# Filter rows and length-64 results fetched for four residues at a time, in a fused spectral filter and MLP-mixer kernel

## The chip, the cores and the metric

The kernel runs on one core of a Trainium2 chip. The metric is the device time of one execution in microseconds (us). TensorE multiplies matrices and accumulates in PSUM; VectorE and ScalarE do elementwise work and can read PSUM; GpSimd does elementwise work in SBUF and issues DMAs; SyncE (SP) only issues DMAs. Each engine works through its own instructions in order and waits on semaphores for the others.

## The reference

The input x has 8 batches of 3008 rows and 256 columns, all in fp32. First each column is filtered in the frequency domain, then a mixer with a token part and a channel part follows:

```
X = rfft(x, axis=1)                      # 1505 frequencies
y = irfft(X * (filt_r + 1j*filt_i), n=3008, axis=1)
h = relu(y^T @ w_tok1) @ w_tok2          # over the 3008 rows: 3008 -> 256 -> 3008
u = y + h^T
out = u + relu(u @ w_ch1) @ w_ch2        # over the columns: 256 -> 1536 -> 256
```

The weights of the mixer come in as 64-bit floats and are turned into fp32 inside the kernel.

## The kernel before

**The transform.** 3008 = 47 x 64, so a transform of length 3008 is done as one of length 64 over rows that lie 47 apart, and one of length 47 for each of its residues. Because the data are real, only the residues k2 = 0 to 31 (with 32 beside 0) are computed. The length-64 result of a batch goes to DRAM (`z_d`). For each residue, z is read back with the 47 positions folded to two halves of 24 rows, multiplied by a small table (`wbi_t`), multiplied by the complex filter rows of that residue, multiplied by a second table, and written to DRAM (`g_d`), from where the mixer reads it.

**Batches.** `GROUPS` holds each batch alone. Batch 0 goes first in a form of its own (`first`), with TensorE to itself. The steps of every later batch b + 1 are generated by `dft` (L561) and woven into the mixer of batch b: `mix` (L1150) yields after each piece of its work, and the loop at the end of the kernel asks a fixed table of places when to take the next step of `dft` (each of which stops at a `yield`). So the order of every engine's instructions is written out by hand and does not depend on times. Batch 1 takes its length-64 transform in twelve plain matmuls; batches 2 to 7 (`tiled`) use sums and differences made by VectorE.

**One length-47 step.** From batch 1 on, a step handles two pairs of residues, that is four residues (`per` is 2, `KC` is 2). `b_pair` (L707) does 16 small matmuls through `four` (L523), eight for each pair, into two PSUM banks. `products` (L715) multiplies both banks by the filter on VectorE, two operations for each bank, one for each pair, since the filter rows of each pair lie in a tile of their own (L721). `join` adds the products to a complex result. `bi_pair` (L729) does the second 16 matmuls, one step later, and SP stores the result. Between the steps lies other work of the mixer. There are eight such steps a batch, seven batches.

**Buffers and SP's order.** `filts` is a ring of three tiles of 128 partitions by 2 (real, imaginary) by 2 by 256. The transform of x uses all of each tile; `filt_pair` (L221) uses only half of it, `[:, :, 0, :]`, with the two residues of the pair in partitions 0 to 63 and 64 to 127. It issues eight DMAs of 24 or 23 rows (L226, L228). Rows between the loaded ones must be zero: `zero_rows` (L587) clears the used half by a memset on GpSimd (L588) when a batch's x is done. `t2_load` (L655) reads z for one pair, four DMAs, eight for the first pair (L667, L668); `w_load` is the table load (L584, one for both pairs) and then `filt_pair`. All of these stand in SP's queue. Ahead of batch 1's first step the order is: table and filter of pair 0, z of pair 0, filter of pair 1, z of pair 1, table and filter of pair 2, z of pairs 2 and 3. Inside the loop a step issues the z reads of the two pairs two steps ahead, and then the filter of pairs three and four ahead.

**The mixer around it.** An item of the channel part is one pair of hidden blocks for 512 rows. `up_first` (L998, matmuls at L1002) fills two banks, ScalarE copies one quarter (L1005), `up_middle` (L1008) adds on VectorE, `up_last` (L1014, matmuls at L1018) reuses the same banks once VectorE has read them, and `down` (L1025, matmuls at L1036) multiplies the item before. All their VectorE sums go through `v` (L979, so their line is L980). `w1_sums` (L819) is a set of GpSimd sums (L829) in the first mixer batch, beside batch 1's transform.

Of the kernel before, what the change touches and what calls it, by code (L numbers as in the profile page):

```python
# [22 lines left out]
D = 256  # L23
P = 128
# [9 lines left out]
XB = 2  # L34
XF = 2 * FB
KC = 2
WC = 2
TI = P - 2 * KH + 1
DT = 256
# [88 lines left out]
def kernel(  # L128
# [53 lines left out]
    def bank(tag):  # L182
        return (psg if tag == "pg" else psum).tile([P, 512], FP32, tag=tag, name="ps_" + tag)
# [34 lines left out]
    def raw(src, row, ap):  # L218
        return bass.AP(tensor=src.tensor, offset=src.offset + row * D, ap=ap)

    def filt_pair(c):  # L221
        t = filts[c % FB]
        for i, src in enumerate((filt_r, filt_i)):
            for odd in range(KC):
                k, to = c * KC + odd, odd * HALF
                nc.sync.dma_start(t[to:to + A, i, 0], raw(src, k, [[64 * D, A], [1, D]]))  # L226
                n, row = (A - 1, 64 - k) if k else (A, 32)
                nc.sync.dma_start(t[to + 32:to + 32 + n, i, 0], raw(src, row, [[64 * D, n], [1, D]]))  # L228

    def filt_load(c):  # L230
        t, k0 = filts_0[c % len(filts_0)], c * KC
# [329 lines left out]
    def dft(bs):  # L561
        first = bs[0] == 0
        nb = len(bs)
        tiled = bs not in GROUPS[0:2]
        per = 1 if first else 2 // nb
        todo = [(b, c) for b in bs for c in range(NXC // 2 if tiled else NXC)]
        wbs = {}
        kept = []
# [1 line left out]
        def table_load(c):  # L570
            if first:
                if c < 5:
                    where, tag = (t1p, "t1") if c > 2 else (wbp, "wb")
                    t = where.tile([P, 2 * P, WC], FP32, tag=tag, name="wb")
                    for h in range(2):
                        nc.gpsimd.memset(t[half_of(h), ts(1 - h, P)], 0.0)
                    kept.append(t)
                wbs[c] = kept[c % 5]
                for h in range(2):
                    nc.sync.dma_start(wbs[c][half_of(h), ts(h, P)], wbi0_d[half_of(h), c])  # L580
            else:
                if c % per == 0:
                    both = wbp.tile([P, per, 4, HALF], FP32, tag="wb", name="wb")
                    nc.sync.dma_start(both, wbi_d[:, c:c + per])  # L584
                    wbs.update((c + j, both[:, j]) for j in range(per))

        def zero_rows(c):  # L587
            nc.gpsimd.memset(filts[c][:, :, 0, :], 0.0)  # L588

        def w_load(c):  # L590
            table_load(c)
            (filt_load if first else filt_pair)(c)

        to_load = list(enumerate(todo))

# [54 lines left out]
                    v = turned.rearrange("p s d -> p d s")[:, d:d + 16, :]  # L650
                    nc.vector.transpose(v, v)
        t2s, t3s, prods = {}, {}, {}
        wide = per * nb

        def t2_load(c):  # L655
            if first:
                return
            if c % per == 0:
                both = t2p.tile([P, per, KC, nb, D], FP32, tag="t2", name="t2")
                t2s.update((c + j, both[:, j]) for j in range(per))  # L660
            for h in range(2):
                z = z_d[place_of[bs[0]][0]].rearrange("(e h k) a b d -> e h a k b d", e=2, h=2)
                for e in range(2):
                    to = t2s[c][ds(h * HALF + e * A, A)]
                    k = c == 0
                    if k:
                        nc.sync.dma_start(to[:, 0:1], z[h, e, :, 0:1])  # L667
                    nc.sync.dma_start(to[:, k:KC], z[e, h, :, c * KC + k:c * KC + KC])  # L668

        def b_unit(k):  # L670
            ps = bank("pg").rearrange("p (b d) -> p b d", b=2)[:, 0:nb, :]
# [25 lines left out]
                           in_=ps.rearrange("p b (g e i) -> p b g e i", e=DH, i=CW))  # L697

        def two_banks(tags):
            return [bank(tag).rearrange("p (b d) -> p b d", b=2)[:, 0:wide, :] for tag in tags]  # L700

        def of(j):
            return slice(j * nb, (j + 1) * nb)

        def b_pair(c):  # L707
            pss = two_banks(turn)
            for j in range(per):
                wb, t2 = wbs[c + j], t2s[c + j]  # L710
                four(lambda h, i: pss[h][half_of(i), of(j)], lambda h, i: wb[half_of(h, KH), i],
                     lambda h, i: t2[half_of(h, KH), i])
            return pss

        def products(c, pss):  # L715
            where = (p1p, p2p)
            for h in range(2):
                prods[c, h] = where[h].tile([P, 2, wide, D], FP32, tag="p%d" % (h + 1), name="p%d" % (h + 1))
                for j in range(per):
                    f = filts[(c + j) % FB][:, :, 0, :].unsqueeze(2).to_broadcast([P, 2, nb, D])  # L720
                    nc.vector.tensor_tensor(out=prods[c, h][:, :, of(j)], in1=f, op=ALU.mult,  # L721
                                            in0=pss[h][:, of(j)].unsqueeze(1).to_broadcast([P, 2, nb, D]))
# [6 lines left out]
        def bi_pair(c, tags):  # L729
            pss, p = two_banks(tags), prods.pop((c, 0))  # L730
            for j in range(per):
                wb = wbs[c + j]
                four(lambda i, h: pss[i][half_of(h), of(j)], lambda i, h: wb[half_of(i), 2 + h],
                     lambda i, h: p[half_of(i), h, of(j)])
            t3 = t3p.tile([P, per * KC, nb, D], FP32, tag="t3", name="t3")
            if per == 1:
                for i in range(KC):
                    by_block(t3[:, i], pss[i])
            else:
                for i in range(KC):  # L740
                    by_block(t3[:, i::KC, 0], pss[i])
            for h in range(2):
                nc.sync.dma_start(g_d[place_of[bs[0]][0]][ds(c * KC, per * KC), ts(h, KH)].rearrange("k r b d -> r k b d"),
                                    t3[half_of(h, KH)])

        if not first:
            for c in range(tiled, FB):
                zero_rows(c)
            for c in range(2 * per):
                if not tiled and c < FB:  # L750
                    w_load(c)
                t2_load(c)
                if tiled and 0 < c < FB:
                    w_load(c)
        yield "w"
        yield "b"
        if not first:
            last = K2 // KC
            for c in range(0, last, per):
                pss = b_pair(c)  # L760
                if c:
                    bi_pair(c - per, ("pg", "pg"))
                products(c, pss)
                for j in range(c + 2 * per, c + 3 * per):
                    if j < last:
                        t2_load(j)
                for j in range(c + min(2 * per, FB), c + min(2 * per, FB) + per):
                    if j < last:
                        w_load(j)
                yield "m"  # L770
                join(c)
                if c + per == last:
                    yield "i"
                    bi_pair(c, turn)
                if c + per < last:
                    yield "b"
            return
        if first:
            for i in range(2):
# [615 lines left out]
```

## Time and profile before

| what | value |
|---|---|
| median of 3 runs | 2410.55 us (2408.51 to 2411.98) |
| the profiled execution, its own time | 2411.46 us |
| its span | 2409.7 us |
| its mean granted TensorE clock | 0.994 |
| TensorE busy | 2363.4 us, 98% |
| VectorE busy | 1954.8 us, 81% |
| ScalarE, GpSimd busy | 689.2 us, 29%; 629.8 us, 26% |
| products with the filter, L721 | 224 operations of 128x512, 0.68 us each |
| filter loads of batches 1 to 7 | 896 DMAs of 24 or 23 KB from SP |
| z reads | 420 DMAs of 48 KB, 56 of 24 KB from SP |

All numbers after the median come from one execution. "Busy" is the sum of the time in which the engine had an instruction in work. A row of the trace in order of time has the start and the duration in us, the engine, the line, the operation, what is written and read, and how many instructions are merged; in square brackets stands how long the engine was idle before it and what released it. Rows of waits read: engine and what it was about to write, its line, what it waited for, us in total, times, longest. "PEld" is the weight load in front of a matmul, "SPq" and "ACTq" are issues of DMAs by SP and ScalarE. A matmul in fp32 appears as two records. The granted clock is the share of full speed that TensorE was given.

### The profile page before, as it was taken

To read this page: it belongs to the slowest core of one execution; us is meant where nothing else is said; L and a number is where in the kernel's file an instruction comes from. 1 tells how busy PE (TensorE), PEld (TensorE's weight loads), DVE (VectorE), ACT (ScalarE), POOL (GpSimd) and SP (SyncE) were. 2 spreads that over 40 slices of the span, in tenths; PEclk is the share of its full clock that TensorE was granted. 3 is DMA by queue.
4 is the path that set the end of the run, shared out by engine and by line. 5 is a ranking of instruction groups with operands and counts; after the bars stand their busy time and mean duration, and the time that the engine had idled before them with its cause. 6 is when DMAs were issued, how large, how long until landed. Compare 5 with 4: busy or idle time off the path is not lost.

```text
span 2409.7 us, 38162 instructions
## 1 busy us (share of the span) xinstructions
PE 2363.4 (98%) x13132; PEld 2013.6 (84%) x13132; DVE 1954.8 (81%) x3781; ACT 689.2 (29%) x1339; POOL 629.8 (26%) x1124
## 2 busy tenths in 40 slices
PE   7988999999999999999999999999999999999998
PEld 4666888888898888988888888988889888898887
DVE  7797887778877888778887788878888788877776
ACT  5732222222223222232222222222222322222222
POOL 7476433211221121112112311221121112112121
PEclk8999999999999999999999999999999999999999
DMA  9973446432353334533345333633235333331100
GB/s 216 234 202 109 137 129 221 126 113 82 112 187 125 90 101 127 182 107 98 101 136 173 105 99 96 196 113 113 86 115 182 122 98 105 111 129 32 39 14 21
DMA packets 195313, 294.37 MB, mean 122 GB/s; under 512 B 40030, under 2 KB 130548, under 8 KB 195120
## 3 DMA queue, kind: packets, MB, share of 16 engines
q1 hardware_dynamic: 153632, 231.26, 30.8%
q0 software_dynamic: 34688, 53.83, 8.4%
q10 hardware_dynamic: 6800, 6.85, 1.0%
q8 instruction: 104, 1.70, 0.3%
q14 instruction: 89, 0.73, 0.1%
HBM read 209.06 MB, written 82.72 MB: 121 GB/s over the span
## 4 chain that ended last, share of the span: by engine, by line
PE 91%; DVE 3%; DMA 2%; issue 1%; POOL 1%; ACT 1%; SPq 0%; DVEq 0%; ACTq 0%; POOLq 0%
PE ps_po L1036 35%; PE ps_pg L1002 20%; PE ps_pg L1018 15%; PE ps_b L523 4%; PE ps_b L866 3%; PE ps_acc L923 3%; PE ps_acc L866 2%; PE ps_pg L523 2%; PE ps_b L923 2%; PE ps_b L901 2%; PE ps_acc L901 2%; DMA st<-in_moe_w_tok_dram 1%; DMA filt<-in_filt_r_dram 1%; DMA x<-in_x_dram 1%; DVE both L279 1%
## 5 line engine op out<-in xcount | busy, mean ns | idle before, releaser
L1044 POOL DMA_DIRECT2D out_dram<-r x752 | 408.2, 550 | 1466.2 <-issue 780.3
L1023 ACT ACTIVATE hh<-hh 128x512 f32<-128x512 f32 (+1 forms) x576 | 347.7, 621 | 1015.7 <-DVE hh L980 1008.2
L980 DVE TENSOR_TENSOR hh<-ps_pg,s 128x512 f32<-128x512 f32 (+3 forms) x864 | 481.4, 585 | 169.3 <-ACT s L1005 159.2
L1036 PE MATMUL ps_po<-t,wc 128*128 128x256 f32 (+1 forms) x2296 | 558.8, 380 | 0.5 <-DVE t L980 0.4
L1036 PEld LDWEIGHTS ps_po<-t,wc 128*128 128x128 f32 x2296 | 427.2, 190 | 96.4 <-issue 39.1
L1002 PE MATMUL ps_pg<-v,wc 128*128 128x256 f32 (+1 forms) x1728 | 412.7, 375 | 1.5 <-POOL wc L381 1.5
L1036 PE MATMUL ps_po<-hh,wc 128*128 128x256 f32 (+1 forms) x1722 | 411.5, 375 | 0.6 <-POOL wc L382 0.6
L1002 PEld LDWEIGHTS ps_pg<-v,wc 128*128 128x128 f32 x1728 | 328.2, 190 | 39.8 <-POOL wc L381 2.3
L1036 PEld LDWEIGHTS ps_po<-hh,wc 128*128 128x128 f32 x1722 | 326.8, 190 | 38.4 <-POOL wc L382 1.4
L1018 PE MATMUL ps_pg<-u,wc 128*128 128x256 f32 (+1 forms) x1152 | 291.9, 376 | 2.5 <-DVE hh L980 2.4
L980 DVE TENSOR_TENSOR t<-t,hh 128x256 f32<-128x256 f32 (+1 forms) x576 | 247.6, 430 | 19.8
L1018 PEld LDWEIGHTS ps_pg<-u,wc 128*128 128x128 f32 x1152 | 216.9, 190 | 34.1 <-DVE hh L980 8.0
L980 DVE TENSOR_TENSOR s<-ps_pg,hh 128x512 f32<-128x512 f32 (+1 forms) x288 | 196.0, 681 | 31.1 <-DVE hh L980 1.4
L1005 ACT COPY s<-ps_pg 128x256 f32<-128x256 f32 (+1 forms) x288 | 105.9, 368 | 337.4 <-PE ps_pg L1002 333.9
L980 DVE TENSOR_TENSOR t<-hh 128x512 f32<-128x512 f32 (+1 forms) x288 | 194.2, 674 | 0.6 <-ACT hh L1023 0.6
L1002 PE MATMUL ps_pg<-u,wc 128*128 128x256 f32 (+1 forms) x576 | 169.9, 377 | 3.9 <-DVE hh L980 3.9
L1018 PE MATMUL ps_pg<-v,wc 128*128 128x256 f32 (+1 forms) x576 | 168.8, 375 | 0.0
L1002 PEld LDWEIGHTS ps_pg<-u,wc 128*128 128x128 f32 x576 | 108.4, 191 | 20.1 <-DVE hh L980 7.8
L1018 PEld LDWEIGHTS ps_pg<-v,wc 128*128 128x128 f32 x576 | 108.9, 190 | 12.9
L980 DVE TENSOR_TENSOR u<-ps_acc,u 128x256 f32<-128x256 f32 (+1 forms) x84 | 46.1, 549 | 71.5 <-PE ps_acc L923 50.5
L980 DVE TENSOR_TENSOR u<-ps_b,u 128x512 f32<-128x512 f32 (+2 forms) x126 | 74.4, 591 | 28.9 <-PE ps_b L923 26.7
L721 DVE TENSOR_TENSOR p<-ps_b,filt 128x512 f32<-128x512 f32 x112 | 72.3, 685 | 16.2 <-PE ps_pg L523 13.4
(164 smaller groups left out, 2700.8 us busy)
## 6 DMA issues: line engine op xcount, KB each, us to landing
w<-w_tmp SPq DMA_DIRECT2D x84, 448.0 KB
w<-w_tmp SPq DMA_DIRECT2D x35, 896.0 KB
out_dram<-r POOLq DMA_DIRECT2D x696, 32.0 KB, 3.8
g_tmp<-t SPq DMA_DIRECT2D x112, 192.0 KB
t<-g_tmp SPq DMA_DIRECT2D x42, 512.0 KB
t<-z_tmp SPq DMA_DIRECT2D x420, 48.0 KB
z_tmp<-t SPq DMA_DIRECT2D x72, 256.0 KB
wb<-wbi_t SPq DMA_DIRECT2D x56, 256.0 KB
```

Source lines behind the costliest of these rows:

```text
L523: nc.tensor.matmul(outs(i, j), stat(i, j), mov(i, j), start=True, stop=True)
L721: nc.vector.tensor_tensor(out=prods[c, h][:, :, of(j)], in1=f, op=ALU.mult, in0=pss[h][:, of(j)].unsqueeze(1).to_broadcast([P, 2, nb, D]))
L866: nc.tensor.matmul(ps[:, at], w[:, n], mov, start=(j == 0 and i in (0, 2)), stop=(j == AP - 1 and i >= 5))
L901: nc.tensor.matmul(ps[:, ds(q * P, n)], t4[b, c][:, r, ts(dh, P)], wai[:, 0:n], start=(first and q == 0), stop=(not first and q == 3))
L923: nc.tensor.matmul(ps[:, ds(j * hw, hw)], h1[:, n, :], w2m[m % 2][:, at, 0:hw], start=(i < 2 and j == 0), stop=(j == len(todo) - 1))
L980: nc.vector.tensor_tensor(out=out, in0=in0, in1=in1, op=op)
L1002: nc.tensor.matmul(ps[:, 0:hw], chan[0][:, jp, n, :], mov, start=True, stop=True)
L1005: nc.scalar.copy(out=s[:, 0], in_=g[0][:, 0, 0:hw])
L1018: nc.tensor.matmul(ps[:, 0:hw], chan[0][:, jp, n, :], mov, start=True, stop=True)
L1023: nc.scalar.activation(out=hs, in_=hs, func=AF.Relu)
L1036: nc.tensor.matmul(po[i][:, j, 0:hw], chan[1][:, jp, n, :], mov, start=(jp == 0 and first == 1), stop=(jp == JP - 1 and last == 1))
L1044: q.dma_start(bass.AP(tensor=ob.tensor, offset=ob.offset + row * D + g * cw, ap=[[N1 * D, 32], [D if h else -D, n], [1, cw]]), blocks[ts(g ...
```

## The change

`filt_quad` takes the place of `filt_pair`: it fills a whole tile of `filts` with the filter rows of four residues, by eight DMAs (ten for the first step), each with two rows for every partition. `zero_rows` clears the whole tile. `t2_load` reads z for four residues by four DMAs (eight for the first step), and the step number `c` counts sets of four. Ahead of the first step and inside the loop the z reads now stand in front of the table and filter loads; the filter is loaded two steps ahead, as z is. `products` makes one operation of 128x1024 for each bank. The matmuls and the stores are as before. `per` and `wide`, which had been there for groups of two batches, are gone. Of the diff, the renaming of `b_pair` and `bi_pair` with the same matmuls is left out:

```diff
+KD = 2 * KC
...
-    def filt_pair(c):
+    def filt_quad(c):
         t = filts[c % FB]
         for i, src in enumerate((filt_r, filt_i)):
             for odd in range(KC):
-                k, to = c * KC + odd, odd * HALF
-                nc.sync.dma_start(t[to:to + A, i, 0], raw(src, k, [[64 * D, A], [1, D]]))
-                n, row = (A - 1, 64 - k) if k else (A, 32)
-                nc.sync.dma_start(t[to + 32:to + 32 + n, i, 0], raw(src, row, [[64 * D, n], [1, D]]))
+                k, to = c * KD + odd, odd * HALF
+                nc.sync.dma_start(t[to:to + A, i], raw(src, k, [[64 * D, A], [KC * D, 2], [1, D]]))
+                down = t[to + 32:to + 32 + A]
+                if k:
+                    nc.sync.dma_start(down[0:A - 1, i], raw(src, 64 - k, [[64 * D, A - 1], [-KC * D, 2], [1, D]]))
+                else:
+                    nc.sync.dma_start(down[:, i, 0], raw(src, 32, [[64 * D, A], [1, D]]))
+                    nc.sync.dma_start(down[0:A - 1, i, 1], raw(src, 64 - KC, [[64 * D, A - 1], [1, D]]))
...
-                if c % per == 0:
-                    both = wbp.tile([P, per, 4, HALF], FP32, tag="wb", name="wb")
-                    nc.sync.dma_start(both, wbi_d[:, c:c + per])
-                    wbs.update((c + j, both[:, j]) for j in range(per))
+                wbs[c] = wbp.tile([P, 2, 4, HALF], FP32, tag="wb", name="wb")
+                nc.sync.dma_start(wbs[c], wbi_d[:, ts(c, 2)])
...
         def zero_rows(c):
-            nc.gpsimd.memset(filts[c][:, :, 0, :], 0.0)
+            nc.gpsimd.memset(filts[c], 0.0)
 
         def w_load(c):
             table_load(c)
-            (filt_load if first else filt_pair)(c)
+            (filt_load if first else filt_quad)(c)
...
         def t2_load(c):
-            if first:
-                return
-            if c % per == 0:
-                both = t2p.tile([P, per, KC, nb, D], FP32, tag="t2", name="t2")
-                t2s.update((c + j, both[:, j]) for j in range(per))
+            t2s[c] = t2p.tile([P, KD, D], FP32, tag="t2", name="t2")
+            z = z_d[place_of[bs[0]][0]].rearrange("(e h k) a b d -> e h a k (b d)", e=2, h=2)
+            k = c == 0
             for h in range(2):
-                z = z_d[place_of[bs[0]][0]].rearrange("(e h k) a b d -> e h a k b d", e=2, h=2)
                 for e in range(2):
                     to = t2s[c][ds(h * HALF + e * A, A)]
-                    k = c == 0
                     if k:
                         nc.sync.dma_start(to[:, 0:1], z[h, e, :, 0:1])
-                    nc.sync.dma_start(to[:, k:KC], z[e, h, :, c * KC + k:c * KC + KC])
+                    nc.sync.dma_start(to[:, k:KD], z[e, h, :, c * KD + k:(c + 1) * KD])
...
         def products(c, pss):
             where = (p1p, p2p)
             for h in range(2):
-                prods[c, h] = where[h].tile([P, 2, wide, D], FP32, tag="p%d" % (h + 1), name="p%d" % (h + 1))
-                for j in range(per):
-                    f = filts[(c + j) % FB][:, :, 0, :].unsqueeze(2).to_broadcast([P, 2, nb, D])
-                    nc.vector.tensor_tensor(out=prods[c, h][:, :, of(j)], in1=f, op=ALU.mult,
-                                            in0=pss[h][:, of(j)].unsqueeze(1).to_broadcast([P, 2, nb, D]))
+                prods[c, h] = where[h].tile([P, 2, 2, D], FP32, tag="p%d" % (h + 1), name="p%d" % (h + 1))
+                nc.vector.tensor_tensor(out=prods[c, h], in0=pss[h].unsqueeze(1).to_broadcast([P, 2, 2, D]),
+                                        in1=filts[c % FB], op=ALU.mult)
...
         if not first:
             for c in range(tiled, FB):
                 zero_rows(c)
-            for c in range(2 * per):
-                if not tiled and c < FB:
-                    w_load(c)
+            for c in range(2):
                 t2_load(c)
-                if tiled and 0 < c < FB:
+                if c or not tiled:
                     w_load(c)
         yield "w"
         yield "b"
         if not first:
-            last = K2 // KC
-            for c in range(0, last, per):
-                pss = b_pair(c)
+            last = K2 // KD
+            for c in range(last):
+                pss = b_sets(c)
                 if c:
-                    bi_pair(c - per, ("pg", "pg"))
+                    bi_sets(c - 1, ("pg", "pg"))
                 products(c, pss)
-                for j in range(c + 2 * per, c + 3 * per):
-                    if j < last:
-                        t2_load(j)
-                for j in range(c + min(2 * per, FB), c + min(2 * per, FB) + per):
-                    if j < last:
-                        w_load(j)
+                if c + 2 < last:
+                    t2_load(c + 2)
+                    w_load(c + 2)
                 yield "m"
                 join(c)
-                if c + per == last:
-                    yield "i"
-                    bi_pair(c, turn)
-                if c + per < last:
-                    yield "b"
+                yield "i" if c + 1 == last else "b"
+            bi_sets(last - 1, turn)
```

More of the change, by code (lines that the diff above doesn't have):

```diff
@@ L564, in dft @@
         tiled = bs not in GROUPS[0:2]
-        per = 1 if first else 2 // nb
         todo = [(b, c) for b in bs for c in range(NXC // 2 if tiled else NXC)]
@@ L652, in dft @@
         t2s, t3s, prods = {}, {}, {}
-        wide = per * nb
         def t2_load(c):
-            if first:
-                return
-            if c % per == 0:
-                both = t2p.tile([P, per, KC, nb, D], FP32, tag="t2", name="t2")
-                t2s.update((c + j, both[:, j]) for j in range(per))
+            t2s[c] = t2p.tile([P, KD, D], FP32, tag="t2", name="t2")
+            z = z_d[place_of[bs[0]][0]].rearrange("(e h k) a b d -> e h a k (b d)", e=2, h=2)
+            k = c == 0
             for h in range(2):
-                z = z_d[place_of[bs[0]][0]].rearrange("(e h k) a b d -> e h a k b d", e=2, h=2)
                 for e in range(2):
                     to = t2s[c][ds(h * HALF + e * A, A)]
-                    k = c == 0
                     if k:
                         nc.sync.dma_start(to[:, 0:1], z[h, e, :, 0:1])
-                    nc.sync.dma_start(to[:, k:KC], z[e, h, :, c * KC + k:c * KC + KC])
+                    nc.sync.dma_start(to[:, k:KD], z[e, h, :, c * KD + k:(c + 1) * KD])
         def b_unit(k):
@@ L699, in two_banks, with b_sets @@
         def two_banks(tags):
[L700 to L708, printed above, removed]
-            for j in range(per):
-                wb, t2 = wbs[c + j], t2s[c + j]
-                four(lambda h, i: pss[h][half_of(i), of(j)], lambda h, i: wb[half_of(h, KH), i],
-                     lambda h, i: t2[half_of(h, KH), i])
+            return [bank(tag).rearrange("p (j d) -> p j d", j=2) for tag in tags]
+        def b_sets(c):
+            pss, wb, t2 = two_banks(turn), wbs[c], t2s[c]
+            for j in range(2):
+                four(lambda h, i: pss[h][half_of(i), j], lambda h, i: wb[half_of(h, KH), j, i],
+                     lambda h, i: t2[half_of(h, KH), j * KC + i])
             return pss
@@ L717, in products @@
             for h in range(2):
-                prods[c, h] = where[h].tile([P, 2, wide, D], FP32, tag="p%d" % (h + 1), name="p%d" % (h + 1))
-                for j in range(per):
-                    f = filts[(c + j) % FB][:, :, 0, :].unsqueeze(2).to_broadcast([P, 2, nb, D])
-                    nc.vector.tensor_tensor(out=prods[c, h][:, :, of(j)], in1=f, op=ALU.mult,
-                                            in0=pss[h][:, of(j)].unsqueeze(1).to_broadcast([P, 2, nb, D]))
+                prods[c, h] = where[h].tile([P, 2, 2, D], FP32, tag="p%d" % (h + 1), name="p%d" % (h + 1))
+                nc.vector.tensor_tensor(out=prods[c, h], in0=pss[h].unsqueeze(1).to_broadcast([P, 2, 2, D]),
+                                        in1=filts[c % FB], op=ALU.mult)
         def join(c):
@@ L727, in join, with bi_sets @@
             nc.vector.tensor_tensor(out=p1[:, 1], in0=p1[:, 1], in1=p2[:, 0], op=ALU.add)
[L729 to L741, printed above, removed]
+        def bi_sets(c, tags):
+            pss, wb, p = two_banks(tags), wbs[c], prods.pop((c, 0))
+            for j in range(2):
+                four(lambda i, h: pss[i][half_of(h), j], lambda i, h: wb[half_of(i), j, 2 + h],
+                     lambda i, h: p[half_of(i), h, j])
+            t3 = t3p.tile([P, KD, D], FP32, tag="t3", name="t3")
+            for i in range(KC):
+                by_block(t3[:, i::KC], pss[i])
             for h in range(2):
-                nc.sync.dma_start(g_d[place_of[bs[0]][0]][ds(c * KC, per * KC), ts(h, KH)].rearrange("k r b d -> r k b d"),
+                nc.sync.dma_start(g_d[place_of[bs[0]][0]][ts(c, KD), ts(h, KH)].rearrange("k r b d -> r k (b d)"),
                                     t3[half_of(h, KH)])
```

## The prediction

> **What bounds the kernel now.** I read the page's busy times first, then the same in stretches of 60 us, because a mean over the span hides where the idle time is.
>
> ```profile
> PE 2363.4 (98%) x13132; PEld 2013.6 (84%) x13132; DVE 1954.8 (81%) x3781; ACT 689.2 (29%) x1339; POOL 629.8 (26%) x1124
> ```
> ```profile
> 180.00:240.00 60.00, 53.05 (x227) 40.13 (x226) 47.95 (x78) 14.39 (x27) 40.29 (x56) 0.94 0.35 108
> 240.00:300.00 60.00, 60.00 (x345) 48.39 (x345) 47.61 (x86) 16.81 (x32) 28.07 (x46) 1.00 0.43 131
> ```
>
> The columns of the stretches are TensorE, weight loads, VectorE, ScalarE, GpSimd, granted clock and DMA. From 240 to 2340 us TensorE is busy 59.98 to 60.00 of every 60: it alone sets the time, and a saving on VectorE or in a DMA queue buys nothing there. Of its 46 idle us 37 lie before 240 us and 9 behind 2400 (the last stores). The edited code first runs near 200 us (batch 1), so only the row 180 to 240 can give anything back: 6.95 us idle, at a mean clock of 0.94.
>
> TensorE's waits in total, its order of time there, and the chain of work:
>
> ```profile
> PE ps_b L523 <- DMA t<-z_tmp: 5.4, 1, 5.4
> ```
> ```profile
> 213.95 1.01 PE L523 MATMUL ps_acc<-t,wb 48*64 48x256 f32 x4
> 220.41 0.69 PE L523 MATMUL ps_b<-t,wb 48*64 48x256 f32 x2 [5.44 <-DMA t<-z_tmp]
> ...
> 221.83 2.07 PE L1036 MATMUL ps_po<-t,wc 128*128 128x256 f32 x4
> ...
> 227.29 1.03 PE L1018 MATMUL ps_pg<-u,wc 128*128 128x256 f32 x4
> ```
> ```profile
> 213.38 2.70 DMA filt<-in_filt_r_dram
> 216.10 4.18 DMA t<-z_tmp
> ```
>
> The first length-64 step of batch 1 does half of its 16 matmuls, then waits 5.44 us, once in the whole run, for the z rows of its second pair of residues. The chain says why those are late: the second pair's filter loads stand ahead of them in SP's queue. SP's own order:
>
> ```profile
> 162.81 0.36 SPq L584 DMA_DIRECT2D wb<-wbi_t  x1
> 206.53 0.31 SPq L226 DMA_DIRECT2D filt<-in_filt_r_dram  x1
> ...
> 209.77 0.30 SPq L667 DMA_DIRECT2D t<-z_tmp  x1
> ...
> 215.65 1.81 SPq L668 DMA_DIRECT2D t<-z_tmp  x4
> ```
>
> SP stands from 163 to 206.5 before a filter load, whose tile GpSimd zeroes only at 205.98. The last write of batch 1's z was issued by ScalarE at 195.57, so the reads could go ten us sooner; the four that matter go at 215.65 to 217.5 and release TensorE at 220.4.
>
> **The stall's second price.** The granted clock is 1.00 until 218, 0.50 to 224.85 and 1.00 after (rows of 1 us: 0.51 at 218, 0.57 at 224). The four L1036 matmuls take 2.07 us instead of 1.03. From 220.4 to 224.85, half of 4.45 us is lost: 2.2.
>
> **The change, part by part.** TensorE's and ScalarE's sequences are the same instructions in the same order, so TensorE can gain or lose by waits alone.
>
> Reads in front, four residues in one: the eight reads of step 0 become the first of SP's instructions after 163. They wait only for z: 195.57 plus a landing of at most 3 us (reads issued by 217.46 released TensorE at 220.4) is 198.5; then 8 x 0.4 us, and the step's table load, now behind them (0.36). All land by about 206; the step begins at 213.24. So the wait goes, even if one of these figures is a few us off.
>
> What is late next is VectorE. Its order there:
>
> ```profile
> 214.26 1.28 DVE L980 TENSOR_TENSOR hh<-ps_pg,s 128x512 f32<-128x512 f32 x2
> 215.46 3.62 DVE L980 TENSOR_TENSOR u<-u,r 128x256 f32<-128x256 f32 x3
> 221.62 1.29 DVE L721 TENSOR_TENSOR p<-ps_b,filt 128x512 f32<-128x512 f32 x2 [2.55 <-issue]
> 222.83 1.28 DVE L721 TENSOR_TENSOR p<-ps_acc,filt 128x512 f32<-128x512 f32 x2
> 225.79 0.42 DVE L980 TENSOR_TENSOR hh<-ps_pg,s 128x256 f32<-128x256 f32 x1 [1.69 <-ACT s L1005]
> ```
>
> It is busy to 219.0 whatever TensorE does. Then come the products, then the hh operation (0.42) that frees the bank for L1018; L1018 follows such an hh at once (hh ends 210.50, L1018 starts 210.54 in the item before). TensorE, unstalled: 16 matmuls from 213.24 in 0.91 us (the same step at 554.13), L1036 x4 with its gap 0.97, L1002 x8 1.72, L1036 x6 1.30: ready for L1018 at about 218.2. VectorE: from 219.0 two products of 1024 elements. Rows: 128x256 0.42 us, 128x512 0.685, so 1.02 ns an element and 1.21 us each; by start to start (0.605 for 512) 1.13, the two 2.26, against 2.40 for the four of now. hh then runs 221.25 to 221.67, and L1018 starts at 221.7, where its weight load now starts at 227.1. **Gain 5.4 us**: gone are 5.44 of wait, 2.2 of half clock and 1.3 in the first half of the step (eight matmuls in 1.72 us that need 0.46, as z rows were just landing); new are 3.5 us of waiting for VectorE. After L1018 the distances between the two engines are those of now (t follows hh by 1.4 us, when L1036 needs it), and TensorE is full from there, so the 5.4 reaches the end.
>
> Longer zeroing: 21 memsets of 1024 elements for 512. On GpSimd 64x1024 costs 0.93 us, 128x512 0.54, so +0.4 to 0.5 each. The three at 206 let filter load 0 go 0.4 us later and push the ten sums behind them (L829, 11.13 us) from 218.5 to 219.9. A rule speaks against this. Row first: beside those sums two t<-t,hh take 2.24 us (0.89 elsewhere), while two hh<-ps_pg,s keep their 1.28. The Trainium skill (GPSIMD Engine Reference, Specifications) says GpSimd shares its SBUF interfaces with VectorE instructions that have two SBUF inputs. By the rule u<-u,r stays slow (3.62 for three) and the products, with one input in PSUM, do not become slow; by the row the third u<-u,r loses 0 to 0.3 us, of which I take none, since it is already slow. Were the products slowed as t<-t,hh is (1.35 us over a pair), the gain would be 4.0.
>
> Filter loads joined (16 issues of 0.25 to 0.30 us a step become 8 of about 0.4, by z's 0.36 to 0.41 for rows twice as long) and z reads joined (8 become 4): SP time alone. Their cover is lead: a step comes every 25 us (554, 579), loads are made two steps ahead, and DMA into filt lands in 2.0 to 8.9 us, median 4.8. Without that lead each late load would hold the step's products. Every residue is loaded at least as early as now (the odd ones a step earlier), and SP no longer waits for the products to free a filter tile. Filter load 0 goes from 207.0 to 211 and lands by 216, or at the worst by 219.9: that would cost 0.9 us.
>
> Products elsewhere: 55 steps each save 0.15 us of VectorE under a full TensorE: 0.
>
> **The sum.** The profiled execution took 2411.46 (span 2409.7), 0.91 over the median 2410.55. 2411.46 - 5.4 = 2406.1; from the median **2405.2**.
>
> **Rivals.** (B) The clock falls in the wait that is left. Rows: idles of 2.1 and 2.2 us (near 149 and 111) kept 1.00; the one of 5.4 lost it after 3.1. Mine is 3.5. The Trainium skill (TensorE: Matmul & The Clock Gate, Part 1) gives a free-running window of about 3.4 us, and half rate after an idle one; the changes at 218.0 and 224.85 lie two such windows apart. By the rows, with the limit between 2.2 and 3.1 us of idle in a window, the clock falls in 20 to 70% of phases; by the rule, which wants the whole window idle, in few. If it falls, L1018 and what follows run at half for some 3.4 us: gain 5.4 - 1.7 = 3.7, time 2406.9.
>
> (C) The reads do not come earlier: a tile still in use, or z landing late, leaves SP standing until 206.5 or longer. For it: a trace names the last waiter only, and SP's was the zeroing. Against: reads issued at 209.77 landed for 213.24, so SP would have to stand ten us more than z needs. Gain 0 to 2, time about 2410.
>
> (D) Slower: a product of 1024 elements costs more than two of 512. Each step has 0.8 us between the hh behind the products (ends 558.99) and L1018's weight load (559.79), so a step's products may grow from 2.40 to 3.2 us for nothing; beyond, each step loses the excess. It decides at 1.7 us an operation: 55 x (3.4 - 3.2) = 11 eats the gain and as much again. At 2.0 us, 55 x 0.8 - 5 = 39 slower, 2449. Against: from 128 to 512 elements these operations lie near one line (0.29, 0.42, 0.61 at 448, 0.685).
>
> **How the numbers follow.** Likeliest 0.55 (2403.5 to 2406.5, with the small terms above as its bounds), B 0.28, C 0.10, D 0.07. A difference of 0.2% is 4.8 us, about what a measurement of this kernel tells from none; its line is 2405.7, just above my number. Faster: 0.44 from the likeliest and 0.06 from B's lower end, 0.50; slower is D, 0.07; the rest 0.43. The range leaves out D, part of C and a little below: 2402.8 to 2410.2.
>
> **What would show it.** No DMA wait at the step near 213; 16 matmuls in a row; z reads issued near 198, ahead of filter loads; L1018 waiting some 3.5 us for VectorE's hh; the clock at 1.00 through 225 (B: 0.50 behind the wait); products of 1.2 us; TensorE full after 240. A product above 1.6 us, a wait for filt, or a TensorE wait after 240 makes me wrong.

## The result, and the profile after

The changed kernel takes 2404.77 us (median of 12 runs, 2403.09 to 2406.63), the kernel before, run beside it, 2410.96 us (12 runs, 2408.51 to 2414.09). The ratio is 0.9975, with an interval of 0.9966 to 0.9984, so 3.9 to 8.2 us less. The prediction was 2405.2.

The profiled execution of the changed kernel took 2404.98 us, its span 2403.2, its mean clock 0.995. The page's busy times, and the two stretches of 60 us (columns as before: TensorE, weight loads, VectorE, ScalarE, GpSimd, clock, DMA):

```profile
PE 2359.4 (98%) x13132; PEld 2012.9 (84%) x13132; DVE 1951.0 (81%) x3669; ACT 689.8 (29%) x1339; POOL 638.3 (27%) x1124
```
```profile
180.00:240.00 60.00, 55.13 (x247) 42.44 (x246) 48.23 (x77) 15.34 (x29) 44.34 (x60) 0.97 0.39 121
240.00:300.00 60.00, 60.00 (x345) 49.13 (x344) 49.59 (x85) 17.45 (x33) 25.43 (x42) 1.00 0.50 152
```

Of these two rows only 180 to 240 changed: 55.13 us busy where there were 53.05, at 0.97 where there was 0.94. From 240 on TensorE's row is as full as it was; that a full row can hide small waits is seen below, under products_longer. VectorE has 112 instructions fewer and 3.8 us less work.

TensorE's order at batch 1's first length-47 step, and its longest wait there:

```profile
211.85 0.43 PE L528 MATMUL ps_b<-t,wb 48*64 48x256 f32 x2
...
212.88 1.13 PE L1011 MATMUL ps_po<-t,wc 128*128 128x256 f32 x4
...
215.57 1.46 PE L1011 MATMUL ps_po<-hh,wc 128*128 128x256 f32 x6
220.25 1.66 PE L993 MATMUL ps_pg<-u,wc 128*128 128x256 f32 x4 [3.22 <-DVE hh L955]
```
```profile
PE ps_pg L993 <- DVE hh L955: 5.6, 4, 3.2
```

Lines have moved: L528, L1011, L977, L993, L955 and L709 are the former L523, L1036, L1002, L1018, L980 and L721. (In the runs further down they move by a few lines again; the four `ps_pg<-u,wc` behind the new wait are the former L1018 everywhere.) Counts of matmuls, here and in the text before, are counts of records: the code of a step's first half has eight matmuls, each of them two records. The 16 small matmuls run without a gap and the wait for z is gone from the list. In its place stands a wait of 3.22 us in front of L993, for the VectorE operation that frees its bank. VectorE at that time, in order:

```profile
212.88 1.28 DVE L955 TENSOR_TENSOR hh<-ps_pg,s 128x512 f32<-128x512 f32 x2
214.08 3.52 DVE L955 TENSOR_TENSOR u<-u,r 128x256 f32<-128x256 f32 x3
217.52 1.21 DVE L709 TENSOR_TENSOR p<-ps_b,filt 128x1024 f32<-128x1024 f32 x1
218.66 1.21 DVE L709 TENSOR_TENSOR p<-ps_acc,filt 128x1024 f32<-128x1024 f32 x1
219.79 0.41 DVE L955 TENSOR_TENSOR hh<-ps_pg,s 128x256 f32<-128x256 f32 x1
```

It has no gap from 212.88 on: TensorE is ready at 217.03 and waits for three slow u<-u,r, two products and one hh. SP and GpSimd show why the z rows are early. SP's order, then GpSimd's:

```profile
160.91 0.25 SPq L518 DMA_DIRECT2D filt<-in_x_dram  x1
198.31 0.30 SPq L663 DMA_DIRECT2D t<-z_tmp  x1
...
201.53 0.35 SPq L587 DMA_DIRECT2D wb<-wbi_t  x1
205.37 0.32 SPq L227 DMA_DIRECT2D filt<-in_filt_r_dram  x1
```
```profile
204.39 2.73 POOL L590 MEMSET filt<- 128x1024 f32 x3
207.09 11.37 POOL L804 TENSOR_TENSOR w<-w 128x384 f32<-128x384 f32 x10
```

The z reads go at 198.31, before the zeroing; the first filter load still follows the zeroing, at 205.37, after the first of the three memsets.

The distance between the two profiled executions can be followed matmul by matmul, as the start before minus the start after. It is 1.39 us at the step's first matmul, 6.83 at the weight load of L993 (227.08 and 220.25), 5.25 at L977 behind it, and 6.4 at the last matmul. So the step itself gave **5.44 us**, and 1.6 of that was lost at once: the granted clock is 0.50 from 220.71 to 224.13. The 1.39 from ahead of the step and some 1.1 in small pieces after it are looked at below. The small pieces lie at four places: 0.42 us at 250 to 257 us of the time of before, 0.27 at 357, 0.33 at 643, 0.17 at 1656. There weight loads wait 0.2 to 0.4 us for VectorE in before and do not in this execution after. One of them, in before:

```profile
642.42 0.73 PEld L1018 LDWEIGHTS ps_pg<-u,wc 128*128 128x128 f32 x4 [0.30 <-DVE hh L980]
```

### The profile page after: what moved, and what is told of

It is laid out like the page before. It is cut to its first block, busy times and chain, and to the rows that moved or that the text cites. A ratio compares the mean times of both kernels' runs of the same rounds, so it can differ in the third digit from the quotient of the medians.

```text
span 2403.2 us, 37053 instructions
## 1 busy us (share of the span) xinstructions
PE 2359.4 (98%) x13132; PEld 2012.9 (84%) x13132; DVE 1951.0 (81%) x3669; ACT 689.8 (29%) x1339; POOL 638.3 (27%) x1124
## 4 chain that ended last, share of the span: by engine, by line
PE 92%; DVE 3%; DMA 2%; issue 1%; POOL 1%; ACT 1%; SPq 0%; ACTq 0%; DVEq 0%; POOLq 0%
PE ps_po L1011 35%; PE ps_pg L977 20%; PE ps_pg L993 15%; PE ps_b L528 3%; PE ps_b L841 3%; PE ps_acc L898 3%; PE ps_acc L841 2%; PE ps_pg L528 2%; PE ps_b L898 2%; PE ps_b L876 2%; PE ps_acc L876 2%; DVE both L284 0%; DVE t L955 0%; DMA g_tmp<-t 0%; DVE both L289 0%
## 5 line engine op out<-in xcount | busy, mean ns | idle before, releaser
L955 DVE TENSOR_TENSOR hh<-ps_pg,s 128x512 f32<-128x512 f32 (+3 forms) x864 | 482.5, 586 | 171.3 <-ACT s L980 161.1
L1011 PE MATMUL ps_po<-t,wc 128*128 128x256 f32 (+1 forms) x2296 | 558.1, 380 | 0.7 <-DVE t L955 0.7
L1011 PEld LDWEIGHTS ps_po<-t,wc 128*128 128x128 f32 x2296 | 427.7, 190 | 95.6 <-issue 38.7
L977 PE MATMUL ps_pg<-v,wc 128*128 128x256 f32 (+1 forms) x1728 | 412.6, 375 | 1.4 <-POOL wc L386 1.4
L1011 PE MATMUL ps_po<-hh,wc 128*128 128x256 f32 (+1 forms) x1722 | 411.5, 375 | 0.6 <-POOL wc L387 0.6
L977 PEld LDWEIGHTS ps_pg<-v,wc 128*128 128x128 f32 x1728 | 327.9, 190 | 39.6 <-POOL wc L386 2.2
L1011 PEld LDWEIGHTS ps_po<-hh,wc 128*128 128x128 f32 x1722 | 326.8, 190 | 38.4 <-POOL wc L387 1.4
L993 PE MATMUL ps_pg<-u,wc 128*128 128x256 f32 (+1 forms) x1152 | 292.3, 376 | 5.7 <-DVE hh L955 5.6
L955 DVE TENSOR_TENSOR t<-t,hh 128x256 f32<-128x256 f32 (+1 forms) x576 | 247.1, 429 | 19.8
L993 PEld LDWEIGHTS ps_pg<-u,wc 128*128 128x128 f32 x1152 | 217.2, 190 | 37.1 <-DVE hh L955 10.8
L955 DVE TENSOR_TENSOR s<-ps_pg,hh 128x512 f32<-128x512 f32 (+1 forms) x288 | 196.1, 681 | 30.0
L980 ACT COPY s<-ps_pg 128x256 f32<-128x256 f32 (+1 forms) x288 | 105.8, 368 | 332.4 <-PE ps_pg L977 329.1
L955 DVE TENSOR_TENSOR t<-hh 128x512 f32<-128x512 f32 (+1 forms) x288 | 194.4, 675 | 0.6 <-ACT hh L998 0.6
L977 PE MATMUL ps_pg<-u,wc 128*128 128x256 f32 (+1 forms) x576 | 169.3, 376 | 3.9 <-DVE hh L955 3.9
L993 PE MATMUL ps_pg<-v,wc 128*128 128x256 f32 (+1 forms) x576 | 169.2, 375 | 0.0
L977 PEld LDWEIGHTS ps_pg<-u,wc 128*128 128x128 f32 x576 | 108.1, 190 | 19.7 <-DVE hh L955 7.5
L993 PEld LDWEIGHTS ps_pg<-v,wc 128*128 128x128 f32 x576 | 109.2, 190 | 13.0
L955 DVE TENSOR_TENSOR u<-ps_acc,u 128x256 f32<-128x256 f32 (+1 forms) x84 | 46.2, 550 | 72.4 <-PE ps_acc L898 50.1
L955 DVE TENSOR_TENSOR u<-ps_b,u 128x512 f32<-128x512 f32 (+2 forms) x126 | 74.5, 591 | 28.8 <-PE ps_b L898 26.7
L898 PE MATMUL ps_acc<-w 128*128 128x256 f32 (+1 forms) x336 | 85.2, 376 | 0.0
```

The lines of the kernel that those rows point to most:

```text
L898: nc.tensor.matmul(ps[:, ds(j * hw, hw)], h1[:, n, :], w2m[m % 2][:, at, 0:hw], start=(i < 2 and j == 0), stop=(j == len(todo) - 1))
L955: nc.vector.tensor_tensor(out=out, in0=in0, in1=in1, op=op)
L977: nc.tensor.matmul(ps[:, 0:hw], chan[0][:, jp, n, :], mov, start=True, stop=True)
L980: nc.scalar.copy(out=s[:, 0], in_=g[0][:, 0, 0:hw])
L993: nc.tensor.matmul(ps[:, 0:hw], chan[0][:, jp, n, :], mov, start=True, stop=True)
L1011: nc.tensor.matmul(po[i][:, j, 0:hw], chan[1][:, jp, n, :], mov, start=(jp == 0 and first == 1), stop=(jp == JP - 1 and last == 1))
```

## The experiments

The ratios are against runs of the kernel before on the same chip: median 2410.95 of 28 runs for the first four kernels below (order_only to matmuls_thrice), 2410.25 of 19 runs for the four with the sums moved, the longer products and the kernel before itself.

### Which part does it: order alone, joining alone, products apart

**order_only** is the kernel before with only the order of SP's reads and loads ahead of batch 1's first step changed:

```diff
-            for c in range(2 * per):
-                if not tiled and c < FB:
-                    w_load(c)
-                t2_load(c)
-                if tiled and 0 < c < FB:
-                    w_load(c)
+            if tiled:
+                ...
+            else:
+                for load, c in ((t2_load, 0), (t2_load, 1), (w_load, 0), (w_load, 1),
+                                (t2_load, 2), (t2_load, 3), (w_load, 2)):
+                    load(c)
```

> The kernel before with one edit: ahead of batch 1's first step the z reads of pairs 0 and 1 stand in front of the table and filter loads; nothing is joined. Theory (the order takes the 5.44 us wait away, VectorE then sets the start of L1018): no wait for z, L1018 starts behind VectorE's hh, four products of 512 in place of two of 1024 cost 0.14 us; 4 to 6 us faster than before, as far as the clock stays or falls. Rival (the joined operations bring the gain): 0 to 1 us faster.

Measured: 2407.19 us (11 runs), ratio 0.9987 (0.9978 to 0.9996), 3.8 us less, a little under the 4 to 6 expected. TensorE's order has the same new wait as the changed kernel, and none for z:

```profile
219.84 2.07 PE L1021 MATMUL ps_pg<-u,wc 128*128 128x256 f32 x4 [3.46 <-DVE hh L983]
```

**joined_old_order** is the changed kernel with the old order ahead of the step (table and filter in front of z):

```diff
             for c in range(2):
+                if not tiled:
+                    w_load(c)
                 t2_load(c)
-                if c or not tiled:
+                if c and tiled:
                     w_load(c)
```

> The changed kernel with one edit: ahead of batch 1's first step each set's table and filter loads stand in front of its z reads again. Theory (what is late next is VectorE, and one joined read brings all four residues): the reads go behind ten filter loads, from about 208 to 211.5 in the changed kernel's time, land by about 214, TensorE waits 2 to 3 us at the step but is still ready for L1018 before VectorE is: as fast as the changed kernel within 1 us, 5 to 6.5 us faster than before. Rival (the order alone does it): the wait is back and it stands at the time of before, 0 to 2 us faster.

Measured: 2409.3 us (11 runs), ratio 0.9993 (0.9984 to 1.0002), 1.65 us less, which is not told apart from nothing. The 5 to 6.5 us of the theory did not come; the rival (0 to 2 us) was right. The wait for z is there, longer than expected. TensorE's order, SP's waits from 204 to 222 us, and SP's order:

```profile
216.10 1.08 PE L528 MATMUL ps_b<-t,wb 48*64 48x256 f32 x3 [4.04 <-DMA t<-z_tmp]
```
```profile
SPq L663 <- DMA filt<-in_filt_r_dram: 1.7, 2, 1.6
SPq L664 <- DMA filt<-in_filt_i_dram: 1.6, 1, 1.6
```
```profile
209.78 0.42 SPq L664 DMA_DIRECT2D t<-z_tmp  x1
211.81 0.30 SPq L663 DMA_DIRECT2D t<-z_tmp  x1
...
213.39 0.37 SPq L663 DMA_DIRECT2D t<-z_tmp  x1
215.40 0.29 SPq L664 DMA_DIRECT2D t<-z_tmp  x1
```

With eight z reads behind ten filter loads, a z read is held twice for 1.6 us until a filter load has landed. The semaphores in the trace say which: this program's DMAs from SP signal on eight semaphores in turn, and each issue waits for the landing of the one eight places ahead. So z reads behind filter loads stand not only in their line of issue but behind their landings. Half as many issues do not remove that; another order does.

**products_split** is the changed kernel with each product of 128x1024 done as two of 128x512:

```diff
-                nc.vector.tensor_tensor(out=prods[c, h], in0=pss[h].unsqueeze(1).to_broadcast([P, 2, 2, D]),
-                                        in1=filts[c % FB], op=ALU.mult)
+                for j in range(2):
+                    nc.vector.tensor_tensor(out=prods[c, h][:, :, j:j + 1], op=ALU.mult,
+                                            in0=pss[h][:, j:j + 1].unsqueeze(1).to_broadcast([P, 2, 1, D]),
+                                            in1=filts[c % FB][:, :, j:j + 1])
```

> The changed kernel with one edit: each product with the filter is again two operations of 512 elements a bank. Theory: VectorE is 8 us longer busy in all, of which 0.14 us lie in front of L1018 in batch 1's first step and the rest under a full TensorE: within 0.5 us of the changed kernel, 5.5 to 6.2 us faster than before. Rival (relief of VectorE brings part of the gain at every step, some 0.02 us in each of 55): 1 to 2 us slower than the changed kernel.

Measured: 2405.5 us (10 runs), ratio 0.9978 (0.9969 to 0.9987), 5.45 us less, 0.7 us short of the changed kernel. Its wait in front of L995 (the same matmul) is 3.35 us. Joining the products is thus worth 0.1 us at this one place, and in the whole nothing that these runs can tell.

So the order of the reads carries the gain: it alone gives 3.8 us, and joining without it nothing that can be told. The intervals of the three gains of 3.8, 5.45 and 6.2 us overlap (1.0 to 5.3, 3.1 to 7.5 and 3.9 to 8.2 us), but 6.2 lies outside that of order_only. Whether joining the loads adds one or two microseconds to the order is not settled.

### What sets the new wait: TensorE given more to do, GpSimd's sums moved

**matmuls_thrice** repeats the 16 small matmuls of the first step twice more, with the same result:

```diff
-            for j in range(2):
+            for j in (0, 1) * (1 if tiled or c else 3):
```

> The changed kernel with one edit: in batch 1's first step the 16 matmuls are done three times, to the same result, which adds about 1.8 us of TensorE's work at that place. Theory (VectorE sets the start of L1018, and TensorE has 3.2 us or more of waiting there): the addition is hidden; the wait shrinks to about 1.6 us, the clock stays at 1.00, and it is as fast as the changed kernel or up to 1.6 us faster. Rival (TensorE itself is on the path there): 1.8 us slower than the changed kernel.

Measured: 2403.52 us (7 runs), ratio 0.9971 (0.996 to 0.9982), 7.4 us less than before: 32 more records of matmuls, and not slower. TensorE's order:

```profile
219.33 1.13 PE L993 MATMUL ps_pg<-u,wc 128*128 128x256 f32 x4 [1.51 <-DVE hh L955]
```

The step started at 210.92, so L993 comes 8.41 us after it, as in the changed kernel (220.25 - 211.85 = 8.40). VectorE alone sets this place. And with 1.51 us of wait instead of 3.22 the clock stays at 1.00.

**sums_spread** is the changed kernel with the `w1_sums` of GpSimd (L804) begun three items later, and two an item instead of six (the stores of these sums move too):

```diff
-            if JP - 2 <= i < JP + 2:
-                for _ in range(6 if i > JP - 2 else 1):
+            if i == JP - 2 or JP + 2 <= i < JP + 10:
+                for _ in range(2 if i > JP - 2 else 1):
                     if w1_todo:
                         w1_todo.pop(0)()
-            elif i >= 2 * JP and i % 2 and w1_out:
+            elif i >= JP + 10 and w1_out:
```

> The changed kernel with one edit: the 16 sums on w1 that GpSimd does right beside batch 1's first step go two at a time into the eight items that follow. Theory (those sums slow VectorE's u<-u,r, and VectorE sets the start of L1018): u<-u,r takes 1.4 us in place of 3.5, the wait for VectorE shrinks by 2.1 us to about 1.2, the clock stays, and three small waits of 0.3 to 0.4 us at that place go: 3 to 6 us faster than the changed kernel, less what the moved sums cost VectorE later. Rival (VectorE is late for another reason): no difference.

Measured: 2403.25 us (6 runs), ratio 0.9969 (0.9958 to 0.9981), 7.0 us less than before and 1.5 less than the changed kernel. VectorE's order, then TensorE's:

```profile
211.80 1.35 DVE L955 TENSOR_TENSOR u<-u,r 128x256 f32<-128x256 f32 x3
214.06 1.23 DVE L709 TENSOR_TENSOR p<-ps_b,filt 128x1024 f32<-128x1024 f32 x1 [0.91 <-DMA filt<-in_filt_r_dram]
```
```profile
216.80 1.13 PE L993 MATMUL ps_pg<-u,wc 128*128 128x256 f32 x4 [0.37 <-DVE hh L955]
```

Without GpSimd's sums beside them the three u<-u,r take 1.35 us instead of 3.52, and the wait falls to 0.37. What is late next is the filter, which now stands behind z: the product waits 0.91 us for it. The sums cost something at their new place. Followed start by start, the lead over the first execution of the changed kernel falls from 5.2 us to 1.3 between 243 and 309 us. The list of TensorE's waits shows 1.1 us of that, for VectorE; its weight loads wait 4.7 us for VectorE there, and a matmul's record can cover such a wait.

**before_sums_spread** makes the same edit in the kernel before, with neither order nor loads changed.

> The kernel before with the same edit as sums_spread. The zeroing no longer stands behind six of those sums, so the filter loads that block SP go ten us earlier and the z reads behind them too. Theory (the wait of before came from SP standing behind a late zeroing): no wait for z at the step, in the old order and with nothing joined; as fast as sums_spread within 1.5 us. Rival (order and joining are needed): 4 us or more slower than sums_spread.

Measured: 2402.2 us (8 runs), ratio 0.9969 (0.9958 to 0.9979), 8.05 us less than before. SP's order and TensorE's:

```profile
159.78 0.36 SPq L584 DMA_DIRECT2D wb<-wbi_t  x1
193.73 0.31 SPq L226 DMA_DIRECT2D filt<-in_filt_r_dram  x1
...
197.85 0.30 SPq L667 DMA_DIRECT2D t<-z_tmp  x1
...
200.84 0.29 SPq L668 DMA_DIRECT2D t<-z_tmp  x1
```
```profile
208.72 0.65 PE L523 MATMUL ps_acc<-t,wb 48*64 48x256 f32 x4
...
213.29 1.03 PE L1018 MATMUL ps_pg<-u,wc 128*128 128x256 f32 x4
```

The zeroing no longer stands behind the sums, SP goes on at 193.73, and with the old order all z reads are out by 201. Neither the wait for z nor that for VectorE is left, and no clock is lost here. Start by start this execution is 5.3 us ahead of the first one of before at the step (3.5 of them at 113 us already, where the kernels do not differ) and 14.0 us at L1018. Further on the sums take back 4.5 us, of which the list of TensorE's waits shows 2.5 (1.5 in front of L1036, 1.0 in front of L1018). This is the least time of all kernels here, by the smallest edit, though its interval overlaps that of the changed kernel.

### How long a product may take

**products_longer** is the changed kernel with the second bank's product done twice, with the same result, in every step:

```diff
-                nc.vector.tensor_tensor(out=prods[c, h], ...
+                for _ in range(1 + h):
+                    nc.vector.tensor_tensor(out=prods[c, h], ...
```

> The changed kernel with one edit: in every step the second bank's product is done twice, to the same result: 1.13 us more of VectorE in each of 56 steps. Theory (0.8 us of slack behind the products, and 0.14 won by joining): each of 55 steps loses 0.2 us and batch 1's first step 1.1: about 12 us slower than the changed kernel. Rival (more slack than I read, TensorE never waits): 1.1 us slower. Rival (no slack): 62 us slower.

Measured: 2433.75 us (4 runs), ratio 1.0096 (1.0082 to 1.011): 29 us more than the changed kernel, more than twice what was expected. In the trace, one step in the middle:

```profile
559.26 2.47 DVE L710 TENSOR_TENSOR p<-ps_acc,filt 128x1024 f32<-128x1024 f32 x2
561.65 0.41 DVE L956 TENSOR_TENSOR hh<-ps_pg,s 128x256 f32<-128x256 f32 x1
```
```profile
560.64 1.46 PE L1012 MATMUL ps_po<-hh,wc 128*128 128x256 f32 x6
562.12 1.13 PE L994 MATMUL ps_pg<-u,wc 128*128 128x256 f32 x4
```

Start by start against the changed kernel's trace, most steps lose 0.38 us, the second and third of a batch 0.43, and the first of each batch 1.0. The added operation is 1.24 us, so the slack is 0.86, 0.81 and only 0.24: a batch's first step has 16 matmuls fewer (the second 16 come one step later), and TensorE reaches L994 that much sooner. A batch loses 1.0 + 2 x 0.43 + 5 x 0.38 = 3.8 us, seven of them 26; batch 1's first step loses another microsecond, since it waits for VectorE already.

Most of this is not seen in TensorE's busy time. Between 320 and 2300 us it is idle for 5.9 us in all (0.1 in the changed kernel), and some 24 us are lost there. The waits stand with the weight loads; those from 240 to 2330 us in front of L993 in the changed kernel, and in front of the same matmuls here (L994), are:

```profile
PEld ps_pg L993 <- DVE hh L955: 2.5, 6, 0.4
PEld ps_pg L994 <- DVE hh L956: 30.7, 61, 1.2
```

### The start of the run, and the clock

**before_again** is the kernel before, unaltered.

> The kernel before, unchanged, for a second profile and as a control of the timing. Every theory: the same time as before within 0.5 us. If the first 113 us (where neither kernel differs) end again near 113.2, the changed kernel's 111.8 there is an effect of the change; if they move by a us or more, it is where the clock's windows fall.

Measured: 2411.72 us (11 runs), ratio 1.0001 (0.9993 to 1.001); the median is 1.5 us above that of the runs beside it. Its first matmuls with g start at 111.90 us, those of the first execution at 113.16. So the time at which batch 0 is done differs between executions of one kernel by 1.26 us, about the 1.39 us that the changed kernel had ahead of its step (111.75 at this place). The kernels do the same up to there, so that part is not counted as the change's. It need not last: before_again runs at half clock from 112.60 to 116.01 us, and its step starts at 213.07, where that of the first execution starts at 213.24. The four executions of the changed kernel reach the step from 2.1 us sooner to 0.2 us later than the first of before.

**after_2, after_3, after_4** are the changed kernel, unaltered, to see its clock again.

> The changed kernel, unaltered, profiled again, to see how its wait of 3.2 us and the clock windows fall together. Theory (the windows of 3.41 us run freely, so their phase at the wait differs between executions): the wait in front of L993 is 3.0 to 3.6 us again, and behind it stands half clock for 3.41 us (1.7 us lost) in some executions, for 6.83 us (3.4 lost) in others, and perhaps none. Rival (the clock's answer is fixed by the program): 3.41 us of half clock again, beginning within 0.5 us of the same place behind the wait.

> The same kernel once more. Theory: the start of the half clock, counted from the start of the wait, differs from the other two executions, and its length is 0, 3.41 or 6.83 us. Rival: the same place and 3.41 us.

> The same kernel once more. Theory: as for the two before; over the four executions at least two different losses of clock at this place. Rival: the same place and 3.41 us in all four.

They took 2406.49, 2402.38 and 2402.04 us (one run each). The wait in front of L993 is the same in all four executions (3.22, 3.23, 3.22, 3.23 us), the clock behind it is not. It is half for 3.41 us in the first two and stays full there in the other two. The rival, a loss fixed by the program, is out. Stretches of 1 us behind the wait, of the first profiled execution of the changed kernel and of after_3:

```profile
220.00:221.00 1.00, 0.75 (x3) 0.64 (x4) 0.90 (x3) 0.00 (x0) 0.00 (x0) 0.86 0.07 24
221.00:222.00 1.00, 1.00 (x4) 0.82 (x3) 0.96 (x2) 0.00 (x0) 0.00 (x0) 0.50 0.65 190
```
```profile
219.00:220.00 1.00, 0.33 (x2) 0.30 (x3) 0.90 (x3) 0.00 (x0) 0.00 (x0) 1.00 0.23 69
220.00:221.00 1.00, 1.00 (x6) 0.74 (x4) 1.00 (x2) 0.00 (x0) 0.00 (x0) 1.00 0.07 25
```

In every trace of this case the clock changes come at whole multiples of 3.413 us from one another. With that grid, one can add up TensorE's idle time in each window and look at the next window's clock. Of 13 traces, the windows up to 240 us that decide it:

| trace | idle in a full-speed window, us | the next window |
|---|---|---|
| after_3, at 217.85 | 1.82 | full |
| changed kernel, at 145.62 | 1.91 | full |
| after_4, at 214.85 | 1.96 | full |
| before_again, at 146.73 | 1.96 | full |
| after_4, at 146.59 | 1.97 | half |
| before_again, at 109.19 | 2.00 | half |
| joined_old_order, at 146.90 | 2.11 | half |
| changed kernel, at 217.30 | 2.95 | half |
| after_2, at 218.24 | 3.09 | half |

From 40 us on all other windows agree: every one with 1.96 us of idle or less is followed by full speed, every one with 1.97 or more by half. A window that is itself at half speed is followed by another half one if it holds 0.61 us of idle or more (six windows), and by full speed at 0.22 or less (sixteen). In the first 40 us the limits are less sharp: one window with 1.86 us (matmuls_thrice, at 17.87) is followed by half, and half windows with 0.44 to 0.51 us by another half one. So a wait of 3.22 us costs nothing where the grid cuts it into 1.4 and 1.8 (after_3), and 1.7 us where 2.95 of it fall into one window. A wait costs about 3 us where its end reaches into the half window, as those of 3.46 and 3.35 us in order_only and products_split do (6.83 us of half clock).

Not each half window costs time. after_3, after_4 and joined_old_order have one near 150 us, behind windows with 2.0 to 2.1 us of idle, and by 160 us after_3 is as far ahead of the first execution as it was at 142 (0.57 and 0.59 us): TensorE waits for VectorE and GpSimd there anyway.

## Why the prediction was right, point by point

- **The wait for z goes, because the reads stand in front.** Right: reads at 198.31 (predicted 198.5), no wait, and order_only shows that the order alone does it. Rival C is out.
- **L1018 follows VectorE, at 221.7.** Right: 220.25 in an execution whose step starts 1.39 us earlier, so 221.64 on the clock of before; 5.44 us gained, where 5.4 was predicted. TensorE is ready at 218.4 on that clock (218.2), and a product takes 1.21 us. matmuls_thrice and sums_spread show the cause: more work for TensorE changes nothing, a faster VectorE does.
- **The rule on shared interfaces against the row.** Weighed rightly: beside the sums u<-u,r took 3.52 us, without them 1.35, while the first product, with one input in PSUM, took 1.21 and 1.23 us. The gain of 4.0 that the row of t<-t,hh would have given did not come.
- **The clock behind the new wait (rival B).** Here the prediction weighed wrongly, although its number held. It took idles of 2.1 and 2.2 us that had kept the full clock for a limit between 2.2 and 3.1 us; in another execution an idle of 2.1 lost it. The limit is near 1.97 us within one window, and a wait of 3.22 us escapes it only where each part is below that. From these numbers, an estimate: the cut must fall between 1.25 and 1.97 us into the wait, 0.72 of 3.41, about 2 in 10 of phases. By this estimate B, given 0.28, was the likelier case. It occurred in two of four executions of the changed kernel, too few to test the estimate, and with it the step's gain was 5.44 - 1.6 = 3.9 us (B said 3.7). The rule of the Trainium skill (TensorE: Matmul & The Clock Gate, Part 1), half rate after an idle window of about 3.4 us, agrees with the runs on the window and its free phase; but in the runs 1.97 us of idle, 58% of a window, were enough.
- **Why the number held all the same.** The terms of the profiled pair are 1.39 ahead of the step, 5.44 in it, -1.6 of clock, and 1.1 to 1.2 in small pieces up to the end, 6.4 in all, as the medians have it (6.2). The first is counted as the start's own spread. The last is the four small places named with the result. The first of them is gained in all four executions of the changed kernel and in order_only, joined_old_order and products_split. The second differs between executions (after_2 waits 0.6 us there). The last two are not gained in order_only, but in the changed kernel, joined_old_order, products_split and sums_spread, and in before_sums_spread too, where nothing is joined. So the waits are known, and why VectorE comes sooner there stays open. The predicted sum is close by luck in part: a term was lost and others won.
- **The 55 other steps give nothing.** Right as far as can be told: what is gained after the step lies at the four small places, not in every step, and products_split is not slower by what can be told. The full rows from 240 us on would not have shown it by themselves.
- **Longer zeroing, joined loads: 0.** Right for what shows: a memset takes 0.95 to 0.97 us instead of 0.52 to 0.55, the sums end at 218.46 (219.85 on the clock of before, predicted 219.9), and no product waits for a filter. sums_spread shows how thin that cover was: with VectorE 2.2 us sooner, the product waits 0.91 for it.
- **Rival D, slower.** It did not happen, since the product costs 1.21 us. Its slack of 0.8 us per step was right for the step that it was read from and wrong for the first of a batch (0.24 over the products of now). Its point of decision stands, as an estimate from these slacks: at 1.7 us an operation a batch would lose (0.98 - 0.24) + 2 x 0.17 + 5 x 0.12 = 1.7 us, seven of them 12, against the 11 that it asked for.

## What to carry to other kernels

When a stall is removed, look at what the next instruction waits for and price that wait from the other engine's own order; here it took back 3.2 of 8.7 us (5.44 gained and 3.22 waited), and the number came out of two lists read side by side. Ask what made the queue late before changing what stands in it: here a zeroing behind a batch of sums held SP, and moving the sums gave as much as the whole change. A slack read from one step of a loop holds for the steps that have the same work, so the first and last are to be read too. An engine that is busy all the time may still be waiting in small pieces: compare two traces start by start, and read the waits of the weight loads, before calling a stretch full.

## What the runs showed of the hardware

- The granted clock follows TensorE's idle time within fixed windows of 3.413 us, whose phase differs between executions: in these traces, from 40 us on, 1.97 us or more of idle in a window halved the next one, and 0.61 us or more kept a half one half. One and the same wait of 3.2 us cost 0 or 1.7 us, one of 3.4 us 3 us. No full-speed window with 1.82 us of idle or less was followed by half speed in any of the 13 traces, so a single wait of that length, with no other idle time beside it, was safe in every phase.
- In this program a DMA issue on SP waits for the landing of the DMA eight places ahead. A small read behind ten loads was held twice for 1.6 us.
- GpSimd sums that read SBUF slow the VectorE operations with two SBUF inputs by a factor of 2.6 (three u<-u,r, 1.35 to 3.52 us; two t<-t,hh, 0.88 to 2.25; each then takes about as long as one of the sums, 1.14 us) and leave those with an input in PSUM alone (two hh<-ps_pg,s of 128x512 take 1.28 us with and without them).
